# Splitting one QK burst into four groups with their own waits and signals, in an attention and state-space kernel

## The chip, the cores and the metric

The kernel runs on one core of a Trainium2 chip. The metric is the device time of one execution in microseconds (us), by the median of the runs; the fast executions of one kernel agree within 0.4%. A core has TensorE (PE; its weight loads are listed as PEld), VectorE (DVE), ScalarE (ACT), GpSimd (POOL) and SyncE (SP). The program gives each its own list of operations and makes them wait for one another by semaphores.

## The reference, cut to what matters

The program computes a gated sum of a state-space layer and of attention with 32 heads over 2048 positions. The change touches the attention.

```python
def _B_ref(x, wqkv, wo):
    B, S, D = x.shape          # 1, 2048, 1024
    H = 32; Dh = D // H        # 32 heads of 32
    ...
    scores = jnp.einsum("bhqd,bhkd->bhqk", q, k) * (Dh ** -0.5)
    p = _softmax(scores, axis=-1)
    o = jnp.einsum("bhqk,bhkd->bhqd", p, v)
    return (...)(o, 0, 2, 1, 3).reshape(B, S, D) @ wo
...
g = _sigmoid((x * gate_w).sum(-1, keepdims=True))
return g * a + (1 - g) * b     # a: the state-space layer, b: the attention
```

## The kernel before

The attention is cut into 512 "bursts". A burst is four heads, two key tiles of 128 and 256 queries. Its eight QK matmuls have only 32 rows, so each head sits in its own 32 rows of the PE array, and four of them run side by side (in the trace they start 3 to 4 ns apart and last 264 to 278 ns each). They fill two of three score slots in PSUM (each slot two banks, one bank per head). ScalarE then takes two exps per burst, z = 0 for heads 0,1 and z = 1 for heads 2,3, each over 128 partitions x 1024 elements. Later bursts do the PV matmuls from the exps' tiles, and between them PE does "dense" matmuls: projections and the whole state-space layer. In 52 of the bursts DVE computes half of the first exp, so that ScalarE's first exp has 512 elements there.

```python
    def burst(self, B):                       # self.p counts bursts
        ...
        sl = [(2 * self.p) % 3, (2 * self.p + 1) % 3]      # two of three slots
        def mm(e):
            m = None
            for kl in range(2):               # key tile
                for h in range(4):            # head
                    kt = 2 * i + kl
                    m = e.matmul(ps[:, 2 * sl[h // 2] + h % 2, 256 * kl:256 * (kl + 1)], K[32 * h:32 * h + 32, ...],
                                 Q[32 * h:32 * h + 32, ...], start=True, stop=True, tile_position=(32 * h, 0))
            return m
        self.S.op("pe", mm, reads=[("K", ...), ("Q", qz)], writes=[("S", sl[0]), ("S", sl[1])], name="qk")
        self.exp(B, 0, sl[0])
        return lambda: self.exp(B, 1, sl[1])
    ...
    def exp(self, B, z, s):
        ...
            self.act(lambda e: e.activation(self.tile[p], ps[:, 2 * s:2 * s + 2, :], ACT.Exp, scale=SCALE),
                     [("S", s)], [("pt", p)], "exp")
    ...
        for p in range(first, NBURST):        # the main loop
            second = self.burst(p)            # QK and the first exp
            ...
            self.pv(head)                     # PV of earlier bursts
            second()                          # the second exp
            ...                               # dense matmuls, PV tail, DVE work
```

`S.op` records an operation with what it reads and writes; from that, a scheduler puts the waits before an operation and, if a later operation of another engine depends on it, one semaphore update at its last instruction. So the one "qk" operation waits until both slots are free before its first matmul, and both exps wait for its eighth matmul. One slot was last read by the second exp two bursts back, the other by the first exp of the burst just before: the first of these ends 0.9 us earlier than the second. `PERIOD` and `DPERIOD` are the lengths of a burst that a small model in the kernel uses to decide where DVE's background work is put into the order; no hardware reads them.

## Time and profile before

| what | before | read from |
|---|---|---|
| time | 940.83 us, median of 3 (940.73 to 942.28) | the runs |
| ACT busy, PE busy | 98%, 95% | the page, part 1 |
| ends of 1024-element exps, one after another | 915 to 918 ns (872 of 972) | instruction records |
| ends of 512-element exps after the one before | mostly 489 to 491 ns | instruction records |
| an exp's recorded length in a steady stretch / when ACT is free | 1330 / 1017 to 1030 ns | instruction records |

From the page of the kernel before: busy time (part 1) and the chain of work that ended last (part 4).

```profile
PE 890.8 (95%) x15095; PEld 501.2 (53%) x15316; DVE 675.6 (72%) x1357; ACT 923.4 (98%) x1034; POOL 9.4 (1%) x39
...
ACT 96%; SPq 1%; DVE 1%; DMA 1%; PE 1%; issue 0%; DVEq 0%
```

ScalarE is busy nearly always and carries the chain. Being busy does not yet tell whether it works at its own speed or is being held up; for that one needs the spacing of its instructions. The view of the exp line in the stretch 314 to 328 us (recorded lengths as minimum/median/maximum in ns):

```profile
L1650 ACT ACTIVATE f_pt<-f_ps x16: 1326/1328/1330, 313.3 to 327.1; 128x1024 bf16<-128x1024 f32 x16
```

An exp is recorded as 1330 ns long, but one ends every 916 ns: the records overlap. Where ScalarE has nothing queued, the same exp is recorded as 1017 to 1030 ns long. The recorded start of a burst's first exp follows the meeting of its wait and not the end of its predecessor: QK's update comes 426 ns after QK's first matmul, the exp's start at 449, while the predecessor still runs. (The second exp's start comes 921 ns after the first's.) So 1330 - 1020 = 310 ns is read as time it spent queued behind its predecessor; the delayed runs below test this reading. The Trainium skill (ScalarE: Activation LUTs, "Step-by-step: what each stage is for") gives 0.833 ns per element, 853 ns for 1024; the trace agrees, with some 63 ns per instruction on top, for 1024 (916) and for 512 (427 + 63 = 490) alike.

The groups of instructions of the QK line and the view of waits, with the idle time of PE's weight loader that is put down to an exp (us in total, times, longest):

```profile
L1634 PE MATMUL f_ps<-f_Q,f_K 32*128 32x256 bf16 x4096 | 203.5, 273 | 15.9 <-ACT f_pt L1650 2.9 <-ACT f_cT_re L1650 2.1 <-ACT f_Et L1650 0.9
...
L1634 PEld LDWEIGHTS f_ps<-f_Q,f_K 32*128 32x128 bf16 x4096 | 61.5, 92 | 177.9 <-ACT f_pt L1650 150.3 <-ACT f_cT_re L1650 7.1 <-issue 4.3
```

```profile
PEld f_ps L1634 <- ACT f_pt L1650: 150.3, 341, 0.9
```

It looks as if PE lost 150 us to waiting for exps, and the change aims at that. The timeline of one steady burst (start, length in us, engine, line, operation; in brackets the idle time before and its releaser):

```profile
318.21 1.02 PE L1416 MATMUL f_ps<-f_xT,f_wb 128*128 128x512 bf16 x4
...
319.29 0.12 PEld L1634 LDWEIGHTS f_ps<-f_Q,f_K 32*128 32x128 bf16 x8 [0.56 <-ACT f_pt L1650]
319.30 0.40 PE L1634 MATMUL f_ps<-f_Q,f_K 32*128 32x256 bf16 x8
319.62 0.47 PEld L1702 LDWEIGHTS f_ps<-f_V,f_pt 128*128 128x128 bf16 x16 [0.21 <-issue]
```

QK begins at 319.30 after a wait for an exp, and the next work on PE follows 0.32 us later. In such a burst (from the instruction records) QK begins 54 ns after the exp's end, and the burst's own first exp begins 449 ns after QK. With the exp's 1330 ns that closes a loop of 1833 ns, the period of a burst. But 310 of it are queueing.

### The profile page before, as it was taken

The page shows a single profiled execution, that of the slowest core. Times are in us where ns is not written, and L with a number is a line of the kernel's source. Part 1 is how long each engine was busy: PE and PEld are TensorE (multiplying, and loading weights), DVE is VectorE, ACT ScalarE, POOL GpSimd, SP SyncE. Part 2 cuts the span into 40 slices and gives each one's busy share as a digit, 9 for nine tenths or more (in the row PEclk, how much of TensorE's full clock was granted, in tenths as well). Part 3 has the DMA queues.
Part 4 walks back from the last instruction along what each step waited for, and adds up shares of the span by engine and source line. Part 5 has one row for each costly group of instructions (what it writes and reads, how often), then busy time and mean ns, then how long its engine had stood idle before and what let it go on. Part 6 is the DMA issues. An engine that isn't in the chain of part 4 may idle for free.

```text
span 938.6 us, 33484 instructions
## 1 busy us (share of the span) xinstructions
PE 890.8 (95%) x15095; PEld 501.2 (53%) x15316; DVE 675.6 (72%) x1357; ACT 923.4 (98%) x1034; POOL 9.4 (1%) x39
## 2 busy tenths in 40 slices
PE   8899999999999999999999999999999999999996
PEld 4555744464444564555644655544654556545553
DVE  2788888888888766657688847568838466766775
ACT  6999999999999999999999999999999999999997
POOL 2000000000000000000000000000000000000000
PEclk9999999999999999999999999999999999999999
DMA  9559433320034002121013300142201212233412
GB/s 199 106 95 144 76 52 76 83 31 27 30 65 93 30 5 52 42 72 31 19 39 59 80 27 30 41 95 53 50 8 41 73 41 87 83 79 115 127 64 74
DMA packets 157076, 60.90 MB, mean 65 GB/s; under 512 B 145664, under 2 KB 145664, under 8 KB 156928
## 3 DMA queue, kind: packets, MB, share of 16 engines
q1 hardware_dynamic: 154768, 58.16, 27.4%
q8 instruction: 121, 1.98, 0.9%
q10 hardware_dynamic: 2160, 0.53, 0.3%
q14 instruction: 27, 0.22, 0.1%
HBM read 16.79 MB, written 12.58 MB: 31 GB/s over the span
## 4 chain that ended last, share of the span: by engine, by line
ACT 96%; SPq 1%; DVE 1%; DMA 1%; PE 1%; issue 0%; DVEq 0%
ACT f_pt L1650 86%; ACT f_OT L1650 2%; ACT f_Et L1650 2%; ACT f_cT_re L1650 2%; ACT f_cT_im L1650 2%; ACT f_ub L1670 1%; SPq L1068 1%; ACT f_hp L1670 1%; DMA f_xT<-in_A_x_dram 1%; ACT f_OT L1670 1%; PE f_ps L1634 0%; PE f_ps L1189 0%; DVE f_xT L1977 0%; PE f_ps L1446 0%; DVE f_xT L1512 0%
## 5 line engine op out<-in xcount | busy, mean ns | idle before, releaser
L1650 ACT ACTIVATE f_pt<-f_ps 128x1024 bf16<-128x1024 f32 x892 | 833.0, 1234 | 0.6 <-PE f_ps L1634 0.6
L1702 PEld LDWEIGHTS f_ps<-f_V,f_pt 128*128 128x128 bf16 x7136 | 228.1, 96 | 115.5 <-issue 93.1
L1702 PE MATMUL f_ps<-f_V,f_pt 128*128 128x33 bf16 x7136 | 279.5, 178 | 0.2 <-ACT f_pt L1650 0.2
L1634 PE MATMUL f_ps<-f_Q,f_K 32*128 32x256 bf16 x4096 | 203.5, 273 | 15.9 <-ACT f_pt L1650 2.9
L1634 PEld LDWEIGHTS f_ps<-f_Q,f_K 32*128 32x128 bf16 x4096 | 61.5, 92 | 177.9 <-ACT f_pt L1650 150.3
L1446 PE MATMUL f_ps<-f_xT,f_wb 128*128 128x512 bf16 x448 | 117.2, 377 | 9.9 <-issue 2.6
L1416 PE MATMUL f_ps<-f_xT,f_wb 128*128 128x512 bf16 x406 | 106.3, 378 | 4.7 <-issue 1.1
L1363 DVE TENSOR_TENSOR_SCAN f_ht<-f_pf,f_init,f_ut 128x512 bf16<-128x512 f32 x64 | 81.1, 1275 | 0.0
L1475 PE MATMUL f_ps<-f_cT_im,f_hp 128*128 128x512 bf16 x190 | 71.8, 378 | 3.6 <-issue 0.7
L1506 PE MATMUL f_ps<-f_wb,f_OT 128*128 128x512 bf16 x218 | 57.8, 378 | 3.0 <-issue 0.2
L1452 DVE CAST f_ub<-f_ps 128x512 bf16<-128x512 f32 x48 | 33.2, 692 | 36.1 <-PE f_ps L1446 36.1
L1434 PE MATMUL f_ps<-f_wb,f_xT 128*128 128x128 bf16 x896 | 59.2, 219 | 0.0
L1446 PEld LDWEIGHTS f_ps<-f_xT,f_wb 128*128 128x128 bf16 x512 | 40.4, 96 | 32.4 <-issue 0.5
L1475 PE MATMUL f_ps<-f_cT_re,f_hp 128*128 128x512 bf16 x146 | 55.1, 378 | 0.2
L1416 PEld LDWEIGHTS f_ps<-f_xT,f_wb 128*128 128x128 bf16 x464 | 36.3, 96 | 28.0
L1434 PEld LDWEIGHTS f_ps<-f_wb,f_xT 128*128 128x128 bf16 x896 | 50.4, 97 | 0.0
L1671 DVE TENSOR_SCALAR f_ut<-f_ps 128x512 int32<-128x512 f32 x26 | 18.0, 692 | 41.1 <-PE f_ps L1634 41.1
L1354 DVE TENSOR_TENSOR f_tq<-f_ht,f_Et 128x512 bf16<-128x512 bf16 x128 | 45.8, 417 | 0.0
L1354 DVE TENSOR_TENSOR f_ut<-f_tq 128x512 f32<-128x512 bf16 x64 | 42.3, 684 | 0.0
L1488 DVE TENSOR_SCALAR f_Ag<-f_ps,f_gcol 128x512 f32<-128x512 f32 x32 | 24.0, 751 | 17.3 <-PE f_ps L1475 17.3
L1354 DVE TENSOR_TENSOR f_tq<-f_ub,f_Et 128x512 bf16<-128x512 bf16 x96 | 34.7, 418 | 0.0
L1423 DVE CAST f_Q<-f_ps 128x512 bf16<-128x512 f32 x30 | 20.8, 692 | 18.3 <-PE f_ps L1416 18.2
(152 smaller groups left out, 843.6 us busy)
## 6 DMA issues: line engine op xcount, KB each, us to landing
ag_scratch<-f_Ag SPq DMA_DIRECT2D x32, 256.0 KB, 2.3
f_hp<-ag_scratch SPq DMA_DIRECT2D x32, 256.0 KB, 2.9
f_wb<-in_B_wqkv_dram SPq DMA_DIRECT2D x21, 256.0 KB, 4.5
out_dram<-f_xT SPq DMA_DIRECT2D x16, 256.0 KB, 2.1
f_wb<-in_B_wo_dram SPq DMA_DIRECT2D x1, 1024.0 KB, 5.3
f_OT<-f_On SPq DMA_TRANSPOSE x63, 2.3
f_wb<-in_B_wo_dram SPq DMA_DIRECT2D x1, 768.0 KB
f_wb<-in_B_wqkv_dram ACTq DMA_DIRECT2D x2, 256.0 KB, 4.4
```

The source lines that it names most:

```text
L1354: ops.append((c, lambda: dve(lambda e: e.tensor_tensor(o, a, b, op), r, w)))
L1363: ops.append((1.29, lambda ri=ri: dve(lambda e: e.tensor_tensor_scan(ht[:, ri, :], rr, ut[:, ri, :], self.init[:, ri, j:j + 1], ALU.mult, ...
L1416: mms.append((1, lambda e, f, l, a=a: e.matmul(ps[:, bank, :], w[:, g % 2, part, a, :], xT[:, a, 512 * ch:512 * (ch + 1)], start=f, stop=l ...
L1434: m = e.matmul(ps[:, bank, 128 * q:128 * (q + 1)], xT[:, a, 128 * kt:128 * (kt + 1)], w[:, g % 2, 2, a, :], start=(a == 0), stop=(a == 7))
L1446: mms.append((1, lambda e, f, l, a=a: e.matmul(ps[:, 7, :], bT[:, n % 2, ri, a, :], xT[:, a, 512 * ch:512 * (ch + 1)], start=f, stop=l), [ ...
L1452: self.dve(lambda e: e.tensor_copy(self.ub[k][:, ri, :], ps[:, 7, :]), [("bank", 7)], [("ub", k, ri)] + over, "evac_u")
L1475: mms.append((1, lambda e, f, l, j=j, ri=ri: e.matmul(ps[:, 7, :], hp[:, ri, j, cols], cT[ri][:, j, 512 * cb:512 * (cb + 1)], start=f, sto ...
L1506: mms.append((1, lambda e, f, l, j=j: e.matmul(ps[:, 7, :], OT[:, j, 256 * qb + 128 * r:256 * qb + 128 * (r + 1)], wo[j][0][:, 512 * cb:51 ...
L1634: m = e.matmul(ps[:, 2 * sl[h // 2] + h % 2, 256 * kl:256 * (kl + 1)], K[32 * h:32 * h + 32, g % 2, 128 * kt:128 * (kt + 1)], Q[32 * h:32 ...
L1650: self.act(lambda e: e.activation(self.tile[p], ps[:, 2 * s:2 * s + 2, :], ACT.Exp, scale=SCALE), [("S", s)], [("pt", p)], "exp")
L1670: self.S.op("act", lambda e: e.activation(t[:, 0, :], ps[:, 2 * s, :], ACT.Exp, scale=SCALE), reads=[("S", s)], writes=[("pt", p)], deps=d ...
L1702: m = e.matmul(ps[:, 6, o:o + 33], self.tile[p][:, h2, 256 * kl + 128 * qt:256 * kl + 128 * (qt + 1)], V[:, g % 2, 2 * i + kl, h, :], star ...
```

## The change

The intent: a matmul needs to wait only if its own slot is still being read, and an exp needs to wait only for its own two heads. So the QK operation becomes four, in the same matmul order: key tile 0 heads 0,1; key tile 0 heads 2,3; key tile 1 heads 0,1; key tile 1 heads 2,3. The first group waits for the exp that ended earlier, the second for the late one; the first exp waits for the third group and the second exp for the fourth.

```diff
-PERIOD = 1.83
+PERIOD = 1.81
-DPERIOD = 1.41
+DPERIOD = 1.40
...
-        def mm(e):
-            m = None
-            for kl in range(2):
-                for h in range(4):
-                    ... (matmul as before)
-            return m
-        self.S.op("pe", mm, reads=[("K", g % 2, i // 2), ("Q", qz)], writes=[("S", sl[0]), ("S", sl[1])], name="qk")
+        for kl in range(2):
+            for z in range(2):
+                def mm(e, kl=kl, z=z):
+                    m = None
+                    for h in (2 * z, 2 * z + 1):
+                        ... (matmul as before)
+                    return m
+                self.S.op("pe", mm, reads=[("K", g % 2, i // 2), ("Q", qz)], name="qk", **{"acc" if kl else "writes": [("S", sl[z])]})
```

Comparing the two programs engine by engine, ScalarE's order is the same, some ten blocks of dense matmuls change places, and some 55 DVE rows move. These moves come from the two periods, not from the split.

More of the change, by code (lines that the diff above doesn't have):

```diff
@@ L1627, in burst @@
         qz, qo = (4 * g + qb // 2) % 5, 256 * (qb % 2)
-        def mm(e):
-            m = None
-            for kl in range(2):
-                for h in range(4):
-                    kt = 2 * i + kl
-                    m = e.matmul(ps[:, 2 * sl[h // 2] + h % 2, 256 * kl:256 * (kl + 1)], K[32 * h:32 * h + 32, g % 2, 128 * kt:128 * (kt + 1)],
-                                 Q[32 * h:32 * h + 32, qz, qo:qo + 256], start=True, stop=True, tile_position=(32 * h, 0))
-            return m
-        self.S.op("pe", mm, reads=[("K", g % 2, i // 2), ("Q", qz)], writes=[("S", sl[0]), ("S", sl[1])], name="qk")
+        for kl in range(2):
[3 more added lines that the diff above has]
+                    for h in (2 * z, 2 * z + 1):
+                        kt = 2 * i + kl
+                        m = e.matmul(ps[:, 2 * sl[z] + h % 2, 256 * kl:256 * (kl + 1)], K[32 * h:32 * h + 32, g % 2, 128 * kt:128 * (kt + 1)],
+                                     Q[32 * h:32 * h + 32, qz, qo:qo + 256], start=True, stop=True, tile_position=(32 * h, 0))
+                    return m
+                self.S.op("pe", mm, reads=[("K", g % 2, i // 2), ("Q", qz)], name="qk", **{"acc" if kl else "writes": [("S", sl[z])]})
         self.exp(B, 0, sl[0])
```

## The prediction

> **What bounds the kernel now.** ScalarE. The page gives ACT 98% busy, PE 95%; the chain that ended last is ACT for 96%, 86% in the exp line. Read instruction by instruction from 10.2 to 933.7 us, the 972 exps of 128x1024 and 54 of 128x512 end at a fixed distance after one another: 915-918 ns for a 1024 exp (also for the second exp of a burst, which has no wait at all), 489-491 ns for a 512 exp. The Trainium skill (ScalarE: Activation LUTs, "The pipeline for one element") gives 0.833 ns per element, 853 ns for 1024; the trace agrees, plus 63 ns per instruction. 972 x 0.9165 + 54 x 0.49 = 917 us. All time that ACT lost above this floor is only 3 to 4.8 us, so no change of PE's waits is worth more than 0.5%.
>
> **What the waits cost now.** The view of waits shows PE waiting 150 us (341 times) for exps before QK. That is not lost: in a steady burst QK starts 54 ns after the exp it waits for ends, the first exp starts 449 ns after QK starts, and takes 1330 ns, where an exp that finds ACT free takes 1017-1030. It queues 310 ns behind its predecessor: the loop exp-QK-exp has 310 ns of slack.
>
> **What the change does.** Matmul order within a burst stays; per engine the order hardly moves (about 10 blocks of dense matmuls swap places, some 55 DVE rows move, from the two altered model periods).
> - The first two matmuls (heads 0,1) wait only for an exp that ended 0.9 us earlier and run before the stall. Then heads 2,3 of key tile 0 and heads 0,1 of key tile 1 share one wave. Where PE was waiting, the first exp can start about 115 ns earlier (waves begin 119 ns apart). ACT is queued there: slack grows to some 425 ns, gain zero.
> - PE gains no throughput: heads 2,3 of key tile 1 still come a wave after the wait, the next matmul still about 330 ns after it.
> - Where ACT does lose time (47-109, 410-428, 591-613, 757-787 us; exps of 1017-1030 ns), PE comes 330-490 ns after the exp's end. It has too much work and doesn't wait. The first exp's last matmul begins at +123 instead of +130 ns: 7 ns, not cumulative. The lost time stays.
> - Added: per burst one satisfiable wait and three semaphore updates on PE, and a wait on each second exp. Exps with and without a wait have the same 916 ns: free. The skill (TensorE: Matmul & The Clock Gate, "The cost: per-tile semaphore tail") has 26 ns per increment; I estimate 0-30 ns in the roughly 70 bursts where PE is that late: 0 to 2 us.
> - Moved dense work: up to 1.5 us either way around 550-620 us.
>
> **On the critical path:** nearly nothing. Head (first exp at 10.2 us) and tail (last 1024 exp ends at 930.2 of 938.6) keep their lengths.
>
> **Predicted:** 940.4 us, 8 in 10 between 938.0 and 942.6. Faster by over 2%: 0.005; within 2%: 0.985; slower by over 2%: 0.01.
>
> **Right if:** PE's wait for exps stays near 150-165 us, now before the heads 2,3 matmuls; steady first exps take about 1440 ns; exp end distances stay 915-918; late stretches are unchanged. **Wrong if:** end distances fall under 910 (ACT was not at its floor); late stretches vanish (PE got faster); or QK of late bursts spreads over more than 330 ns (waits break the packing of row tiles).

## The result, and the profile after

Ratios here are those that the record gives for the fast runs of the two kernels, with their intervals; they are not quite the ratios of the medians that are quoted.

| | median us | range | ratio to before, 95% interval |
|---|---|---|---|
| before | 940.87 (4 runs: the three above and one more) | 940.73 to 942.28 | |
| after | 940.69 (4 runs) | 939.95 to 941.90 | 0.9996 (0.9979 to 1.0013) |
| after, again in later rounds | 939.28 (5 runs; before 940.32, 9 runs) | 938.93 to 940.66 | 0.9993 (0.9979 to 1.0006) |

The time is the same. The profile looks different at first. The page of the changed kernel, parts 1 and 4:

```profile
PE 925.4 (99%) x15316; PEld 520.3 (55%) x15316; DVE 674.1 (72%) x1357; ACT 923.2 (98%) x1034; POOL 10.0 (1%) x39
...
PE 61%; ACT 36%; SPq 1%; DMA 1%; issue 0%; DVE 0%; DVEq 0%
```

PE seems to have become the bound: 99% busy and 61% of the chain. Neither reading holds. Of the 34.6 us that PE's busy time grew by, 23.6 also appear in a run with the old QK (914.4 us for the new periods alone, with 15316 records too): the trace of before lacks 221 matmul records. The rest goes with PE's stall, which now lies inside QK. And the chain of the same kernel is ACT 98% in a run where only one of the waits differs (the exps' own, below), at the same time.

The exp line of the changed kernel in the same stretch, then QK's groups:

```profile
L1651 ACT ACTIVATE f_pt<-f_ps x17: 1374/1408/1412, 312.7 to 327.3; 128x1024 bf16<-128x1024 f32 x17
```

```profile
L1635 PE MATMUL f_ps<-f_Q,f_K 32*128 32x256 bf16 x4096 | 230.3, 273 | 3.8 <-ACT f_cT_re L1651 1.2
...
L1635 PEld LDWEIGHTS f_ps<-f_Q,f_K 32*128 32x128 bf16 x4096 | 80.3, 92 | 158.5 <-issue 73.0
```

The exps now queue 390 ns instead of 310: they are ready 82 ns earlier and end no earlier. The ends of the 1024-element exps are still 914 to 919 ns apart. The weight loader's idle time before QK is still 158.5 us (177.9 before), although QK's first matmuls now hardly wait (0.15 us, below). So this idle time does not measure a stall. The view of waits of the changed kernel, then a burst of the kernel before whose named exp had ended 470 ns before QK began:

```profile
PEld f_ps L1635 <- issue: 73.0, 192, 0.4
PEld f_ps L1635 <- ACT f_pt L1651: 57.6, 143, 0.6
```

```profile
590.80 0.12 PEld L1634 LDWEIGHTS f_ps<-f_Q,f_K 32*128 32x128 bf16 x8 [0.42 <-ACT f_pt L1650]
```

The timeline of the changed kernel shows where the stall went:

```profile
318.57 0.25 PEld L1635 LDWEIGHTS f_ps<-f_Q,f_K 32*128 32x128 bf16 x8 [0.42 <-issue]
318.57 0.53 PE L1635 MATMUL f_ps<-f_Q,f_K 32*128 32x256 bf16 x8
...
319.03 0.47 PEld L1703 LDWEIGHTS f_ps<-f_V,f_pt 128*128 128x128 bf16 x16 [0.21 <-issue]
```

QK now takes 0.53 us instead of 0.40, because two matmuls begin early and the other six come after the stall. The next work on PE comes as late as before.

Two sums from the instruction records say the same. PE's true stall is the distance from the matmul before QK to QK's first, less the distance that QK has when it doesn't wait (311 ns after a 512-column matmul, 151 after a 128-column one, 110 after PV), plus what QK is spread beyond 130 ns. Over the 448 bursts from 123 to 923 us:

```
                          stall before QK   stall inside QK   bursts without a stall
before                        24.1 us            0.05 us              201
after                          0.15 us          24.05 us              201
```

And the time that ScalarE lost against a floor of 915 and 488 ns per exp, by stretch of the span (the first 40 us, 0.1 to 0.2 us, are only in the sum; the sums contain some 1.7 us of 1 to 2 ns steps over the floor):

```
                   all     40-80 us   80-330   330-550   550-740   740-950
before            4.77       0.82      0.99      0.74      1.06      1.08
after             4.51       0.41      0.99      0.72      1.16      1.06
split alone       4.70       0.81      1.00      0.72      1.04      1.05
periods alone     4.51       0.43      1.00      0.74      1.19      1.07
```

The only part that shrank, 0.4 us between 40 and 80 us, belongs to the periods.

### The profile page after: what moved, and what is told of

It is laid out like the page before. It is cut to its first block, busy times and chain, and to the rows that moved or that the text cites. A ratio compares the mean times of both kernels' runs of the same rounds, so it can differ in the third digit from the quotient of the medians.

```text
span 939.2 us, 33706 instructions
## 1 busy us (share of the span) xinstructions
PE 925.4 (99%) x15316; PEld 520.3 (55%) x15316; DVE 674.1 (72%) x1357; ACT 923.2 (98%) x1034; POOL 10.0 (1%) x39
## 4 chain that ended last, share of the span: by engine, by line
PE 61%; ACT 36%; SPq 1%; DMA 1%; issue 0%; DVE 0%; DVEq 0%
ACT f_pt L1651 33%; PE f_ps L1703 17%; PE f_ps L1635 13%; PE f_ps L1446 9%; PE f_ps L1475 9%; PE f_ps L1416 8%; PE f_ps L1434 4%; ACT f_ub L1671 1%; SPq L1068 1%; ACT f_cT_re L1651 1%; DMA f_xT<-in_A_x_dram 1%; ACT f_Et L1651 1%; ACT f_cT_im L1651 1%; PE f_ps L1481 1%; ACT f_OT L1651 0%
## 5 line engine op out<-in xcount | busy, mean ns | idle before, releaser
L1635 PE MATMUL f_ps<-f_Q,f_K 32*128 32x256 bf16 x4096 | 230.3, 273 | 3.8 <-ACT f_cT_re L1651 1.2
L1635 PEld LDWEIGHTS f_ps<-f_Q,f_K 32*128 32x128 bf16 x4096 | 80.3, 92 | 158.5 <-issue 73.0
L1446 PE MATMUL f_ps<-f_xT,f_wb 128*128 128x512 bf16 x512 | 131.0, 377 | 0.3
L1416 PE MATMUL f_ps<-f_xT,f_wb 128*128 128x512 bf16 x464 | 119.0, 378 | 0.0
L1475 PE MATMUL f_ps<-f_cT_re,f_hp 128*128 128x512 bf16 x192 | 72.6, 378 | 0.1
L1506 PE MATMUL f_ps<-f_wb,f_OT 128*128 128x512 bf16 x252 | 65.7, 379 | 0.1
L1354 DVE TENSOR_TENSOR f_tq<-f_ub,f_Et 128x512 bf16<-128x512 bf16 x96 | 34.6, 417 | 0.0
```

The source lines that it names most:

```text
L1354: ops.append((c, lambda: dve(lambda e: e.tensor_tensor(o, a, b, op), r, w)))
L1416: mms.append((1, lambda e, f, l, a=a: e.matmul(ps[:, bank, :], w[:, g % 2, part, a, :], xT[:, a, 512 * ch:512 * (ch + 1)], start=f, stop=l ...
L1446: mms.append((1, lambda e, f, l, a=a: e.matmul(ps[:, 7, :], bT[:, n % 2, ri, a, :], xT[:, a, 512 * ch:512 * (ch + 1)], start=f, stop=l), [ ...
L1475: mms.append((1, lambda e, f, l, j=j, ri=ri: e.matmul(ps[:, 7, :], hp[:, ri, j, cols], cT[ri][:, j, 512 * cb:512 * (cb + 1)], start=f, sto ...
L1506: mms.append((1, lambda e, f, l, j=j: e.matmul(ps[:, 7, :], OT[:, j, 256 * qb + 128 * r:256 * qb + 128 * (r + 1)], wo[j][0][:, 512 * cb:51 ...
L1635: m = e.matmul(ps[:, 2 * sl[z] + h % 2, 256 * kl:256 * (kl + 1)], K[32 * h:32 * h + 32, g % 2, 128 * kt:128 * (kt + 1)], Q[32 * h:32 * h + ...
```

## The experiments

The theory: ScalarE's own speed is the floor; the loop exp-QK-exp has 310 ns of slack and the split only adds to it. The rivals: (1) the split and the moved work each change the time and cancel; (2) PE is the bound, as the chain after says; (3) the loop of waits sets the period of a burst; (4) the added waits and updates cost PE time that is hidden; (5) the split gives PE time that is hidden. Measured times are medians with their number of executions; "before" is the kernel before in the same rounds.

### The changed kernel again, the split alone, the periods alone

```diff
 # split alone: the changed kernel with
-PERIOD = 1.81
+PERIOD = 1.83
-DPERIOD = 1.40
+DPERIOD = 1.41
 # periods alone: the kernel before with the opposite edit
```

> The changed kernel once more, in five rounds beside the kernel before. Floor theory (ScalarE ends 1024-wide exps 916 ns apart whatever PE's waits are): ratio to before 0.999 to 1.001. Rival 1 (split and new periods each move time, and cancel): the same here; the next two runs decide. Rival 2 (the run-to-run spread of 1 us comes from the granted PE clock in the first and last microseconds, not from the change): times of both kernels follow the granted clock of the run, about 0.5 us more per 0.001 less clock.

> The split QK with the old periods 1.83 and 1.41, so that no dense matmul and no DVE instruction changes its place. Floor theory: 940.6 us, within 0.7 of before. Rival 1 (a gain by the split is given back by the moved work, or the reverse): differs from before by 1.5 us or more, with the opposite sign in the run with the periods alone.

> The old QK with the new periods 1.81 and 1.40. Floor theory: within 1 us of before; the stretch of late exps near 590 us moves by some 10 us as in the changed kernel. Rival 1: differs by 1.5 us or more, opposite to the split alone.

Measured, with before at 940.32 us (9 runs): changed kernel 939.28 (ratio 0.9993, 0.9979 to 1.0006), split alone 940.07 (5 runs; 0.9995, 0.9982 to 1.0009), periods alone 940.32 (5 runs; 0.9999, 0.9986 to 1.0013). Rival 1 falls: neither part moves the time by as much as 0.2%. Whether the changed kernel is 0.5 us faster, as its 0.4 us of less lost time would have it, is not clear of the noise.

The guess about the PE clock ("rival 2" in the first of these expectations; in the others rival 2 is that PE is the bound) holds in part. In the profiled runs the core's last microseconds differ: where the granted clock fell to 0.5 for one window of 3.4 us at 926.9 to 928.5 us (after, periods alone, heads first, the first delayed run), the end comes 9.06 to 9.47 us after the last 1024-element exp; where it did not (before, after again, split alone, the two halves below), 8.27 to 8.52 us. That is about 1 us. The window lies over the end of the last exp there: a dense matmul shows 634 ns in it for 378, and the last PV matmul starts 0.95 us later after that exp than in the kernel before. The changed kernel has profiles of both kinds. "0.5 us per 0.001 of clock" is not borne out run by run: at 0.998, runs of before took 940.01 to 940.57 us.

### Is the slack real? Delaying the first exp by 185 and by 385 ns

```diff
 # the kernel before; from burst 16 on the first exp also waits for the first (third) PV group after QK
-            second = self.burst(p)
+            exp0, second = self.burst(p)
...
-            self.pv(head)
+            self.pv(head[:1])      # second run: head[:3]
+            exp0()                 # deps = [the last PE operation so far]
+            self.pv(head[1:])      # second run: head[3:]
```

> The kernel before, but from burst 16 on the first exp of a burst waits until the first PV group after QK is done too: by the semaphore updates in the trace of before that is 185 ns after QK's own. No instruction is added or moved on PE. Floor theory with 310 ns of slack: less than 1.5 us slower; first exps of steady bursts then take about 1145 ns instead of 1330. Rival 3 (the loop exp-QK-exp is what sets a burst's 1833 ns): 185 ns on about 440 bursts, 60 to 90 us slower.

> As the delayed run before it, but the first exp waits for the third PV group after QK, 385 ns after QK's own update. That is 75 ns over the slack of 310 ns that the exps' durations show. Theory: the loop is now the bound, 54+835+1020 = 1909 ns per burst instead of 1833: 25 to 40 us slower, first exps take 1017-1030 ns nearly everywhere, PE's stall grows by as much. If the slack was larger than read (400 ns or more): under 3 us slower. If there is none: 150 us or more.

Measured: delayed by 185 ns, 940.96 us (4 runs; ratio 1.0005, 0.9990 to 1.0021). Delayed by 385 ns, 977.51 us (4 runs; before 940.59; ratio 1.0391, 1.0375 to 1.0407). The exp line in 314 to 328 us, of the first and of the second run:

```profile
L1656 ACT ACTIVATE f_pt<-f_ps x17: 1141/1142/1147, 313.3 to 328.0; 128x1024 bf16<-128x1024 f32 x17
```

```profile
L1656 ACT ACTIVATE f_pt<-f_ps x16: 1017/1021/1025, 313.2 to 327.6; 128x1024 bf16<-128x1024 f32 x16
```

A delay of 185 ns comes off the queueing (1330 to 1146 ns) and off nothing else. A delay of 385 ns uses up the 310 and leaves 75 ns per burst: 36.9 us over 496 bursts are 74 ns each. The exps then find ScalarE free (1017 to 1025 ns). So the slack is as large as the exps' lengths say, and rival 3 falls for the kernel as it is: in it, the loop doesn't set the period. The second delay makes it do so.

### What if ScalarE is no longer the bound? Narrow exps

```diff
 # before and after alike; wrong on purpose (it still passed the comparison with the reference)
-ACT.Exp of self.tile[p] <- ps[:, 2 * s:2 * s + 2, :]
+ACT.Exp of self.tile[p][:, :, 0:448] <- ps[:, 2 * s:2 * s + 2, 0:448]
 # PV reads its last 128 columns from 320 on instead of 384
```

> The kernel before with every full exp cut from 1024 to 896 elements (448 per head) and PV's last block read 64 columns earlier; the result is wrong on purpose, all instructions of PE and their order stay. By the 0.833 ns per element and 63 ns of the traces an exp then needs 810 ns, a burst 1620. PE needs 1833 less the stall of 24.1 us over 448 bursts, about 1780 ns. Floor theory: ScalarE releases, PE takes over: 914 us, 908 to 920, PE's stall before QK near 0. Rival 2 (the kernels are bound by PE, as the chain of the changed kernel says with 61%): 938 to 941.

> The changed kernel with the same narrow exps: what the split is worth, and what its added wait and three updates per burst cost, where PE is the bound. Theory (same PE work, satisfied waits are free, signals do not hold PE up): within 2 us of the narrow kernel before. Rival 4 (the added waits and updates cost PE 20 ns or more a burst, hidden so far): 8 us or more slower than it. Rival 5 (the split gives PE time): 5 us or more faster than it.

Measured: narrow before 926.52 us (4 runs; ratio to before 0.9850, 0.9835 to 0.9865), narrow after 925.33 us (5 runs; 0.9840, 0.9826 to 0.9853). The busy time of the narrow kernel before, and its exp line in 314 to 328 us:

```profile
PE 877.0 (95%) x15095; PEld 503.9 (54%) x15316; DVE 675.3 (73%) x1357; ACT 866.0 (94%) x1034; POOL 9.3 (1%) x39
```

```profile
L1650 ACT ACTIVATE f_pt<-f_ps x16: 911/912/918, 313.4 to 327.2; 128x896 bf16<-128x896 f32 x16
```

Shortening the exps makes both kernels faster, so PE was not the bound of either: rival 2 falls. With ScalarE relieved, it no longer queues (an exp of 896 elements on a free engine should take an estimated 1020 - 128 x 0.833 = 913 ns), and PE's stall for exps, before and inside QK, is 2.2 and 2.0 us instead of 24: PE's own work and its waits for others than exps set the time. There the changed kernel is 1.2 us faster in the medians. The intervals of the ratios overlap, but the times do not (926.42 to 926.97 against 925.19 to 926.11), so a gain of some 0.1% is likely; whether it is the split's or the periods' was not separated. So the split neither costs PE 20 ns a burst (rival 4: 8 us) nor gives it time worth 5 us (rival 5).

My 914 us were a miss: 926.5. The sum took all 24 us of stall for a gain. Part of it turned into another wait. The dense matmuls share one PSUM bank, and the first of a new chain must wait until DVE has emptied it. From the weight loads' records between 123 and 900 us, the time by which the first dense load comes late after PV is 7.6 us in the kernel before and 19.8 us in the narrow one: 12.2 us that had been hidden behind the exps. Those late loads start 41 to 42 or 104 to 105 ns after an update by DVE, in both kernels.

### Each half of the split alone

```diff
 # the changed kernel. Half 1: early matmuls, but both exps wait for the fourth group
-**{"acc" if kl else "writes": [("S", sl[z])]}
+**(dict(writes=[("S", sl[z])]) if not kl else dict(acc=[("S", sl[0]), ("S", sl[1])] if z else []))
 # Half 2: one wait for both slots first, but each exp waits for its own heads
+**({"acc": [("S", sl[z])]} if kl or z else {"writes": [("S", sl[0]), ("S", sl[1])]})
```

> First half of the change alone: heads 0,1 of key tile 0 run before the stall, but both exps wait for the burst's last group. Theory: 939 to 941.5 us. In steady stretches the last group's update comes some 67 ns after the third group's (trace of the changed kernel), so a first exp starts 80 ns earlier than there is no need to: it takes about 1345 ns, near the 1330 of before and not the 1412 of the changed kernel. Rival 1 (each half moves time): 1.5 us or more off.

> Second half alone: one wait for both slots ahead of all eight matmuls, but each exp waits for its own heads. Theory: 939 to 941.5 us. The third group's matmuls then fall in the second wave, 7 ns before the last; with the 17 ns that late bursts of the changed kernel show, first exps of steady stretches take about 1347 ns. So the 82 ns of slack that the change brought need both halves together. Rival 1: 1.5 us or more off.

Measured, with before at 940.33 us (7 runs): half 1 939.58 us (4 runs; ratio 0.9991, 0.9974 to 1.0008), half 2 939.79 us (4 runs; 0.9998, 0.9981 to 1.0014). First exps of steady bursts take 1347 and 1346 ns. The exp line of half 1 in 314 to 328 us:

```profile
L1651 ACT ACTIVATE f_pt<-f_ps x16: 1332/1342/1347, 313.4 to 327.1; 128x1024 bf16<-128x1024 f32 x16
```

So each half alone adds 16 or 17 ns of slack, both together 82. Only if heads 0,1 of key tile 0 have already run can heads 0,1 of key tile 1 share the first wave after the stall, and only if the exp waits for just that group does it see it. The page of half 1 has the chain that I set against the "PE 61%" above:

```profile
ACT 98%; DMA 1%; PE 0%; DVE 0%; issue 0%; SPq 0%; DVEq 0%
```

Two kernels of the same time, one with the chain on PE and one with it on ScalarE. The chain steps back from an exp's recorded start to what released it. In the changed kernel that is a matmul that no longer waits for an exp, so the walk stays on PE, although the exp then lay queued for 390 ns. That is my reading of how the view works; that the view's share does not tell the bound is what the runs show.

### Heads 0,1 first

```diff
 # the changed kernel, the groups in another order
-        for kl in range(2):
-            for z in range(2):
+        for z in range(2):
+            for kl in range(2):
```

> The changed kernel with the four groups in another order: both key tiles of heads 0,1 first, then both of heads 2,3. So nothing of the first exp waits for the exp just before: the loop is relieved completely. But the second group must wait about 110 ns for its own rows of the array, and a burst's QK needs three waves, about 450 ns in place of 330. Theory: the loop had slack, PE had only some 54 ns per burst (24.1 us over 448 bursts): 55 to 65 ns slower per burst, 20 to 35 us slower, 960 to 975. Rival 3 (waiting for exps is what costs): same or faster.

Measured: 940.85 us (4 runs; before 940.59; ratio 0.9999, 0.9984 to 1.0014). Here nothing of the first exp waits for the exp just before, the queueing grows up to 470 ns (recorded lengths up to 1492 ns), and the time is the same: more slack is worth nothing. The exp line in 314 to 328 us:

```profile
L1651 ACT ACTIVATE f_pt<-f_ps x17: 1375/1450/1492, 312.8 to 327.3; 128x1024 bf16<-128x1024 f32 x17
```

The expectation of 20 to 35 us slower was wrong in its mechanism. A late burst (one that waits for nothing) in this run, starts in ns from QK's first matmul; PE's updates from the same zero:

```
matmul starts:        0    4 |  14   17 | 120  123 | 134  136
PE's updates:       301, 410, 453, 495
next PE matmul:     336     (changed kernel: 329)
```

Program order is heads 0,1, then heads 0,1 of the other key tile, then heads 2,3 twice. The second pair can't begin 14 ns after the first on the same rows, since it begins 120 ns after it in every other order. So the matmuls at 14 and 17 are those of heads 2,3, which PE ran ahead of the second group. The updates bear it out: had the second group's matmuls been those at 14 and 17, its update would have come about 43 ns after the first; it came 109 ns after, 287 ns after the matmul at 123. The trace has a more direct sign. The first load of heads 2,3 is the one that carries the second wait for an exp. Of the 447 bursts from 123 to 923 us it is the third load to start in 175, and there the third matmul starts some 15 ns after the first; in 216 it is the fifth, as in program order. PE filled the free rows, kept the updates in program order, and lost 7 ns instead of 110.

### Where the split would pay: the loop alone

These two programs have no PV and no dense work, only QK, two exps and filler matmuls per burst, in sections with joined and with split QK. Their outputs are wrong, which doesn't matter for the times.

> The loop alone, output wrong on purpose: QK bursts, two exps each, three slots, one 512-wide matmul as filler, no PV and no dense work; four sections of 48 bursts. Joined QK with 1024-wide exps and split QK with 1024-wide exps: both 1833 ns per burst, the floor of ScalarE (2 x 916). Then exps of 512 elements, whose floor is 2 x 490 = 980 ns and which take 597 ns alone: joined QK 54+449+597 = 1100 ns (the loop binds), split QK 421+597 = 1018 ns (421 ns from an exp's end to the next first exp's start in the changed kernel). If the split gave nothing even where the loop binds: 1100 in both. If it gave the 115 ns of my prediction: 985.

> The loop alone again, output wrong on purpose, because the first one ran at half the PE clock for most of its time (joined 1320 ns, split 1190 ns per burst with 512-element exps at half clock; only 26 split bursts came at full clock, 993 ns). Here PE is warmed up longer and each burst has 512+384 columns of filler[...]; four sections of 72 bursts, the 512-element exps first. At full clock: joined QK 54+449+597 = 1100 ns, split QK 993 ns as in the 26 bursts, floor 980. With 1024-element exps 1833 ns in both. If the split's gain at half clock was an artefact of the clock: 1100 in both.

In the first program PE ran at half the granted clock (0.5) for most of its time. With 512-element exps it showed 1320 ns per joined burst; the split bursts at half clock had 1107 to 1273 ns, and the 26 at full clock 993. So the joined 1100 ns were missed there, and no pair at the same full clock was had. The second program got it: at full clock, joined 1101 to 1102 ns, split 993 ns, in 72 bursts each. The timeline of PE's QK in the joined section, then in the split one:

```profile
30.27 0.40 PE L238 MATMUL m_ps<-m_Q,m_K 32*128 32x256 bf16 x8 [0.22 <-ACT m_pt L242]
...
31.38 0.40 PE L238 MATMUL m_ps<-m_Q,m_K 32*128 32x256 bf16 x8 [0.22 <-ACT m_pt L242]
...
32.48 0.40 PE L238 MATMUL m_ps<-m_Q,m_K 32*128 32x256 bf16 x8 [0.22 <-ACT m_pt L242]
```

```profile
119.81 0.58 PE L238 MATMUL m_ps<-m_Q,m_K 32*128 32x256 bf16 x8
...
120.80 0.58 PE L238 MATMUL m_ps<-m_Q,m_K 32*128 32x256 bf16 x8
...
121.80 0.58 PE L238 MATMUL m_ps<-m_Q,m_K 32*128 32x256 bf16 x8
```

Bursts are 1.10 us apart joined and 0.99 split: 10% of a burst, where the loop binds. The split bursts come near ScalarE's floor of 2 x 490 = 980 ns but do not reach it: their first exps still last 597 to 599 ns, as on a free engine, and start 395 ns after the end of the exp before (395 + 598 = 993). The loop still sets the period.

The first program's expectation had 421 ns there, from the changed kernel, and so 1018. The 26 ns lie in the signals. In the small programs no other engine waits for the first two groups, so a split burst has two updates and not the four of the changed kernel, and the third group's update comes 318 ns after the second group's first matmul instead of some 343. With four updates the split would be worth an estimated 84 ns here (1102 - 1018) and not 109. The last two sections, with 1024-element exps, had 1833 ns per burst in both forms, and that at half the PE clock: QK was slower (matmuls of 387 to 417 ns in the first program, 264 to 278 at full clock), the exps queued only some 90 ns joined and 305 split (recorded lengths 1112 and 1326 ns), and still not a nanosecond was lost. Half the PE clock ate most of the slack and left the time alone.

### What is left open

That the changed kernel is faster by 0.4 us or so is likely from the lost time between 40 and 80 us and not shown by the times. Why a section of the small programs drops to half the PE clock was not looked into. A version that beats both kernels was not found: each of the seven full kernels without a forced delay or narrowed exps lies between 939.3 and 940.9 us.

## Why the prediction was right

- **The time.** 940.4 us was forecast, with 938.0 to 942.6; measured 940.69 and, again, 939.28 us. Right: the floor of ScalarE holds in both kernels, exps of 1024 elements end 914 to 919 ns apart, and the delayed run (185 ns, no cost) and the narrow exps (14 us faster) show from both sides that this, and not the waits, sets the time.
- **The floor.** Right in size. Two of the "54 of 128x512" are copies in the tail and not exps, 1 us of the 917.
- **The slack of 310 ns.** Right, to a few ns: 185 ns of delay cost nothing, 385 ns cost 74 ns per burst.
- **The first exp 115 ns earlier, slack 425 ns, exps of 1440 ns.** Right mechanism, size off: 82 ns, some 390 ns, 1412 ns. The term that was mis-sized is the signal. The third group's matmuls start 7 ns after the second group's, but its update lands 42 ns later (in one steady burst the four updates come 301, 438, 480 and 547 ns after QK's start). In late bursts the 7 ns were 17: the single update of before comes 427 ns after QK's start, the third of four at 410. The small programs say where most of it goes: with no update at the second group, the first exp starts 108 ns earlier (395 instead of 54 + 449 after an exp's end), close to the 115.
- **PE gains no throughput.** Right: the next matmul comes as late as before, the stall is 24.1 us before and 24.2 after, and with PE as the bound both kernels have nearly the same time.
- **PE waits 150 us for exps.** A wrong reading, without consequence for the time. The view counts idle time of the weight loader, which is idle some 0.4 us before QK even where nothing is waited for. In the kernel before, the burst at 590.80 us has "0.42 <-ACT" although the exp named had ended 470 ns earlier. PE's true stall was 24 us. "PE's wait for exps stays near 150-165 us" therefore failed as a test: 57.6 us are now put down to exps and 73.0 to issue, for a stall of the same size.
- **Late stretches unchanged.** Right for the split alone. In the changed kernel the part between 45 and 62 us went, and the one from 591 us on begins at 573; in the run with the periods alone at 571. So both moves belong to the periods.
- **Head and tail keep their lengths.** The first exp starts at 9.97 us (10.17 before). From the last 1024-element exp to the end it is 9.47 us in one profile of the changed kernel and 8.32 in the other (8.42 before): the window of half clock, not the change.
- **Added waits and updates, 0 to 2 us.** Nothing of it shows: where PE is the bound the changed kernel is not slower. **Moved work, up to 1.5 us either way:** the periods alone have a ratio of 0.9999.

## What to carry to other kernels

Here, how much longer an exp was recorded than on a free engine was the slack of the loop that feeds it (310 ns read; 185 ns of delay cost nothing, 385 cost 74): read such a difference before taking waits away upstream. Finer waits shortened a loop of dependences here, so they paid where the loop set the period (1102 to 993 ns with half-size exps) and nothing where an engine in the loop was at its own speed (1833 ns in both). Neither a large sum of waits nor a chain that moves to another engine is evidence of a bound; delaying the suspected step by a known amount, below and above the supposed slack, is.

## What the Trainium skill lacked or had wrong

- TensorE: Matmul & The Clock Gate, "The mechanism" (packing of small matmuls), says that matmuls start and end strictly in program order, and that weight loads can be pulled ahead. With the groups in the order heads 0,1 twice, then heads 2,3 twice, matmuls of the later group started 14 and 17 ns after the first while the earlier group's started at 120 and 123; the semaphore updates came in program order. Here the matmuls went ahead with their loads (175 bursts). The recorded ends are modelled and show nothing either way.
- The same page, "The cost: per-tile semaphore tail", has 26.3 ns per increment and 4.7 ns per tile, an estimated 36 ns for each further pair of tiles with one increment. Here updates of pairs whose last matmuls start 7 ns apart came 42 to 43 ns apart.
- Perfetto Trace Analysis, "DVE / Act Engine Instruction", says that the recorded start of a ScalarE instruction is when it begins to execute. In steady stretches of the two kernels a first exp's is 22 to 24 ns after the semaphore update that it waited for, while the predecessor still runs: the same exp is recorded with 1017 to 1492 ns. No page says that the difference can be read as slack.
- ScalarE: Activation LUTs, "Step-by-step: what each stage is for", has the 0.833 ns per element. The same page's "What ACT_TABLE_LOAD costs" has 186 ns + 0.833 ns per element with immediate scale and bias, and an overlap of 93 ns back to back: an estimated 946 ns for 1024 elements. Here it is 63 ns + 0.833 per element: 916 ns for 1024, 809 for 896, 490 for 512 elements. Whether the difference comes from reading PSUM was not tested.
- TensorEngine Tiling (Array Packing), "Key Properties", says that a change of the tiling mode drains PE, without a number. From a 512-column dense matmul to the next dense one it is 215 ns here, to QK 311. The 96 ns more go with the switch; its share was not separated from that of QK's wait.
- TensorE: Matmul & The Clock Gate, "What's actually happening", has the free-running window of 3413 ns; the trace agrees (half-clock records of 3413 ns). It doesn't say what it does to a comparison: with such a window over the end of the last full exp, the same kernel ended about 1 us later (9.47 against 8.32 us after that exp). In the run delayed by 385 ns the window was over 1.0 us before that exp's end, and the rest took 8.52 us.
